# Streaming and retrieval attention into a Swish layer: unit 1 in the packed form of the later units, with a new hand-fixed order

## The chip, the cores and the metric

The kernel runs on one core of a Trainium2 chip. The metric is the time of one execution on the device in microseconds (us). A core has a matrix engine (TensorE, PE in the profile; PEld is its weight load), a vector engine (VectorE, DVE), an activation engine (ScalarE, ACT), a general engine (GpSimd, POOL) and a queue that issues DMAs (SyncE, SP). Each takes its instructions strictly in program order and waits at the first one whose inputs or buffers are not ready.

## The reference

```
scores = q @ k.T / 8                 # batch 4, 8 heads, 768 positions, head size 64
mask   = causal                      # heads 0, 2, 6 ("retrieval")
         causal & (key < 4 or query - key < 64)      # heads 1, 3, 4, 5, 7 ("streaming")
a = softmax(where(mask, scores, -1e9));   y = a @ v
x = y as (4*768, 512);  h = x @ w_in (512 x 2048);  g = h * sigmoid(beta * h)
out = g @ w_out (2048 x 512)
```

All arrays are float32 in memory; the kernel computes in bf16 with float32 sums.

## The kernel before

**Units.** Work is cut into eight units, unit n = 2b + u for batch b and half u of 384 query rows. Each unit loads its part of q, k and v, casts it to bf16, turns q and k (by PE for units 0 to 3, by DMA transposes in blocks for units 4 to 7), forms scores in "rounds" of two PSUM banks, takes exponentials on ACT, masks them on DVE or POOL, sums them and multiplies by v on PE (`pv`, two halves g per unit), and normalises into `xT` on DVE. A streaming head needs only a band: for each chunk of 64 queries two blocks of 64 keys, plus the four sink keys.

**Two forms.** Units 0 and 1 ("early") use five plain rounds for heads 0 and 2, one for heads 1 and 3, one for heads 4 and 5, and rounds for heads 6 and 7 plus a round "k" of sink scores: eleven rounds in unit 1. Their reciprocals are spread over rows by four matmuls (`spread`). From unit 2 on (`n >= RD`) the "packed" form puts several heads' pieces into rounds of up to 512 columns, eight rounds in an odd unit and four in an even one. There the sink keys sit in the oldest rows of a band's own key block: `kp_copy` makes such key blocks (KP), `qd_copy` a copy of head 6 on other partitions (QD), `sink_v` copies the sink rows of v into the shifted and plain v tiles, and three small "edge" DMAs (`load_edge`) bring the v rows that those displaced. Reciprocals R of units 2 to 7 go over DRAM: sums `sc`, turned by DMA into `rec`, reciprocal on DVE, written to `rd`, read back spread over partitions as R.

**The Swish layer.** For each unit `first` runs 16 steps of four matmuls of 384 columns (w_in tile s), each followed by a tanh on ACT (`t`) and a product on DVE (`gT`); `second` runs 48 matmuls of 512 columns (w_out tile 0 to 15, three output row groups) in groups of three. Weights come in four loads of 1 MB for w_in and four for w_out, each cast by POOL in four tiles. PSUM has two pairs of banks for scores (`sp`) and a ring of four banks (`b`). Three staging tiles (`wf`) hold weight loads and the q, k and v blocks of 256 KB (three DMAs to a block triple).

**The order.** Each piece of work is added to a plan with an engine, a cost, what it needs and gives, and ring slots. `SEQUENCE` lists the pieces' numbers in the order in which they are planned and `CHOICE` picks an engine for those that may run on several; `run` gives each piece the planned start that its engine, inputs, slots and a model of the DMA bus allow, and the program is emitted in the order of those starts. So on each engine the order of `SEQUENCE` is the program order, and the costs only place engines against each other and set how many filler matmuls unit 0 gets (`fill`).

Of the kernel before, what the change touches and what calls it, by code (L numbers as in the profile page):

```python
# [19 lines left out]
NQ = 384  # L20
# [4 lines left out]
RD = 2  # L25
KD = 256
# [69 lines left out]
]  # L96
CHOICE = (
    "aagaagaadgaddadadddddgdggdddddaaggaagddagaaddddadaddagdddddaaddggdaaagaggddaadadggggadggaddgggaddgag"
    "daaadaadaadddaaaaaaddddaddaa"
# [102 lines left out]
def kernel(  # L202
# [78 lines left out]
    esk_1, sink_sel = KP[0][:, 0:NQ], KP[2][:, 96:192]  # L281
    blk = KP[1][0:96, 0:NQ].rearrange("p (c n) -> p c n", n=W)
# [97 lines left out]
    def const_blk(eng):  # L380
        cast(eng, blk, sel_k6.unsqueeze(2).to_broadcast([96, CK, W]))
# [116 lines left out]
    def sink_copy(b):  # L498
        VE[b] = vp.tile([128, H - 1, D], BF16, name="VE", bufs=RINGS["VE"])
        dve.tensor_mul(VE[b][0:96], held.pop("sinks")[0:96, D:].rearrange("p (h d) -> p h d", d=D),  # L500
                       sink_own[:, 1:].unsqueeze(2).to_broadcast([96, H - 1, D]))
# [119 lines left out]
    def packed(n):  # L621
        return n >= RD

    def rounds_of(pi, n):
# [31 lines left out]
        def band(h):  # L656
            if n >= RD:
                return strip(h, CK * u, CK * (u + 1), 0)
# [9 lines left out]
        if pi == 3:  # L668
            r = plain(a)
            if u == 0:  # L670
                return [(r[0], band(b)), (r[1], kk)]
# [327 lines left out]
    def pv(x, g):  # L999
# [8 lines left out]
        for t in (2 * g, 2 * g + 1):  # L1008
# [3 lines left out]
            for i, h in enumerate(XT[t] if x.n else (2 * t, 2 * t + 1)):  # L1012
# [14 lines left out]
                else:  # L1027
# [7 lines left out]
                    if x.n < 2:  # L1035
                        continue
# [407 lines left out]
```

## Time and profile before

| | us |
|---|---|
| median of 3 runs | 232.65 (232.5 to 233.43) |
| profiled execution, whole | 233.11 |
| its span from first to last instruction | 231.4 |
| PE busy | 221.7 |
| DVE busy | 154.4 |
| ACT busy | 143.2 |
| POOL busy | 91.0 |

The profile is one execution. Every instruction goes through one helper line (L118), so groups are told apart by tiles: `b<-xT,w_in` is the first product, `b<-w_out,gT` the second, `sp<-QK` scores, `sp<-es,vb` P·V, `b<-es,two` and `b<-es,one` the sums. In a timeline row the first number is the start and the second the length; in brackets stands the time that the engine was idle before it and what ended that. Matmuls are pipelined, so a row's length is longer than the distance to the next one, and costs are read from starts.

### The profile page before, as it was taken

What the parts mean: (1) busy time and instruction counts of PE and PEld (TensorE: products, weight loads), DVE (VectorE), ACT (ScalarE), POOL (GpSimd) and SP (SyncE); (2) the same over time, 40 slices, a digit from 0 to 9 for tenths busy, and PEclk for the clock granted to TensorE, in tenths of its full rate; (3) what the DMA queues carried; (4) which work ended last, traced back from release to release, by engine and by line L of the source; (5) the groups of instructions that cost most, each with busy time, mean ns of one, the idle gap of its engine ahead of it and who ended that gap; (6) DMA issues with size and microseconds to landing.
All of it is one profiled execution on the core that took longest, in us unless ns stands there. A gap on an engine that the chain in (4) does not pass through costs nothing.

```text
span 231.4 us, 6505 instructions
## 1 busy us (share of the span) xinstructions
PE 221.7 (96%) x2577; PEld 128.8 (56%) x2600; DVE 154.4 (67%) x372; ACT 143.2 (62%) x233; POOL 91.0 (39%) x233
## 2 busy tenths in 40 slices
PE   8889999999999979999999999999999999999995
PEld 8656666665544535565555456645555555465543
DVE  5787789877376188886669377764885475467630
ACT  5899988887736158825885277537749445008601
POOL 4717876896763924528453535073000000000000
PEclk9999999999999999999999999999999999999999
DMA  6999999998889999997999899974500015402012
GB/s 188 289 274 358 375 238 323 379 338 203 193 177 224 257 192 216 235 196 142 221 210 217 210 216 252 199 142 126 150 3 0 3 48 146 138 0 91 3 45 91
DMA packets 84264, 42.28 MB, mean 183 GB/s; under 512 B 66042, under 2 KB 77002, under 8 KB 84234
## 3 DMA queue, kind: packets, MB, share of 16 engines
q1 hardware_dynamic: 83962, 41.67, 74.0%
q8 instruction: 20, 0.33, 0.6%
q10 hardware_dynamic: 272, 0.20, 0.3%
q14 instruction: 10, 0.08, 0.1%
HBM read 32.27 MB, written 6.37 MB: 167 GB/s over the span
## 4 chain that ended last, share of the span: by engine, by line
PE 62%; DMA 18%; SPq 7%; POOL 6%; issue 2%; DVE 2%; ACT 1%; POOLq 0%; DVEq 0%
PE b L118 55%; SPq L118 7%; PE sp L118 7%; DMA q2f<-in_q_dram 4%; DMA vf<-in_v_dram 4%; DMA wf<-in_moe_w_out_dram 3%; DMA wf<-in_q_dram 3%; DMA R<-rd 3%; POOL w_out L118 2%; POOL w_in L118 2%; DMA rec<-sc 1%; DVE xT L118 1%; POOL KP L118 1%; POOL c L118 1%; ACT es L118 1%
## 5 line engine op out<-in xcount | busy, mean ns | idle before, releaser
L118 DVE SCALAR_TENSOR_TENSOR gT<-t,b 128x384 bf16<-128x384 f32 x128 | 69.3, 552 | 37.7 <-ACT t L118 32.7
L118 PE MATMUL b<-xT,w_in 128*128 128x384 bf16 x512 | 90.2, 326 | 1.7 <-DVE xT L118 1.6
L118 ACT ACTIVATE t<-b,beta_h 128x384 f32<-128x384 f32 x128 | 72.7, 582 | 28.2 <-PE b L118 22.0
L118 PE MATMUL b<-w_out,gT 128*128 128x512 bf16 (+2 forms) x377 | 85.4, 370 | 2.2 <-issue 1.4
L118 PEld LDWEIGHTS <-w_in 128*128 128x128 bf16 x512 | 48.5, 98 | 36.6 <-issue 1.9
L118 PEld LDWEIGHTS <-gT 128*128 128x128 bf16 x400 | 37.2, 98 | 40.0 <-issue 0.8
L118 ACT ACTIVATE es<-sp 128x1024 bf16<-128x1024 f32 (+4 forms) x50 | 46.0, 945 | 9.4 <-PE sp L118 9.2
L118 ACT ACTIVATE osb<-b 128x512 f32<-128x512 f32 (+2 forms) x14 | 7.9, 567 | 33.3 <-PE b L118 30.8
L118 POOL CAST c<-wf 128x256 bf16<-128x256 f32 x48 | 18.0, 413 | 24.0 <-DMA wf<-in_k_dram 13.4
L118 DVE TENSOR_TENSOR xT<-sp,R 64x384 bf16<-64x384 f32 (+4 forms) x30 | 16.0, 554 | 7.4 <-DMA R<-rd 5.1
L118 POOL COPY KP<-QK 128x24 bf16<-128x24 bf16 (+5 forms) x48 | 11.5, 287 | 18.9 <-DMA QK<-c 15.4
L118 PE MATMUL sp<-QK 64*64 64x64 bf16 (+7 forms) x432 | 17.4, 234 | 0.8 <-ACT es L118 0.7
L118 PEld LDWEIGHTS <-QK 64*64 64x64 bf16 (+1 forms) x432 | 11.0, 105 | 9.4 <-issue 7.5
L118 DVE TENSOR_TENSOR es<-es,mask_c 128x256 bf16<-128x256 bf16 (+3 forms) x39 | 11.6, 315 | 4.7 <-ACT es L118 4.6
L118 POOL CAST vb<-wf 128x512 bf16<-128x512 f32 x18 | 12.1, 690 | 6.5 <-DMA wf<-in_v_dram 6.4
L118 DVE COPY QK<-b 128x384 bf16<-128x384 bf16 (+1 forms) x14 | 8.9, 641 | 7.3 <-PE b L118 7.2
L118 PE MATMUL sp<-es,vb 128*64 128x64 bf16 (+5 forms) x240 | 13.5, 235 | 0.0
L118 DVE TENSOR_SCALAR osb<-b 128x512 f32<-128x512 f32 x11 | 7.5, 680 | 8.4 <-PE b L118 8.4
L118 DVE TENSOR_TENSOR es<-es,mask_s 128x128 bf16<-128x128 bf16 (+7 forms) x28 | 11.9, 438 | 0.0
L118 PEld LDWEIGHTS <-vb 128*64 128x64 bf16 x252 | 11.3, 111 | 0.9
L118 DVE COPY vs<-vb 64x1536 bf16<-64x1536 bf16 (+4 forms) x19 | 9.8, 522 | 1.1 <-POOL vb L118 0.5
L118 POOL CAST w_in<-wf 128x512 bf16<-128x512 f32 x16 | 9.7, 631 | 1.7 <-DMA wf<-in_moe_w_in_dram 1.6
(108 smaller groups left out, 197.2 us busy)
## 6 DMA issues: line engine op xcount, KB each, us to landing
out_dram<-osb SPq DMA_DIRECT2D x23, 256.0 KB, 5.4
wf<-in_v_dram SPq DMA_DIRECT2D x18, 256.0 KB, 4.9
wf<-in_moe_w_in_dram SPq DMA_DIRECT2D x4, 1024.0 KB
wf<-in_moe_w_out_dram SPq DMA_DIRECT2D x4, 1024.0 KB
R<-rd SPq DMA_DIRECT2D x9, 384.0 KB, 5.2
q2f<-in_q_dram SPq DMA_DIRECT2D x16, 192.0 KB, 4.4
wf<-in_q_dram SPq DMA_DIRECT2D x12, 256.0 KB, 5.3
wf<-in_k_dram SPq DMA_DIRECT2D x12, 256.0 KB, 4.7
```

The costliest lines, as they stand in the source:

```text
L118: ins = f(*a, **k)
```

## The change

Unit 1 takes the packed form (`FD = 1`: bands, sinks, KP, QD and edge rows), while its sums and reciprocals stay those of the early units (`n < RD`); its eight rounds are planned as single steps (`SD = 2`), not as bursts of two. The sink scores and the "own" sink rows of v are left to unit 0. The even units' four rounds are cut anew: the bands of heads 4 and 5 leave the first two rounds, so these need no KP, and the masks of the four rounds become 15 instructions instead of 9. A constant (`blk`) moves from a KP tile to an output staging tile. In the plan a block triple is priced at 4.25 instead of 3.65 (q, k) and 3.6 (v), a q/k load at 0.65 instead of 0.62. `SEQUENCE` and `CHOICE` are new throughout.

```diff
+FD = 1
+SD = 2
 SEQUENCE = [
...
 CHOICE = (
...
-        return n >= RD
+        return n >= FD
...
             if pi == 0:
...
-                        ([full(a, 1, 0)] + strip(4, 2, CK, 256), [full(b, 1, 0)] + strip(5, 2, CK, 256))]
+                        ([full(6, 0, 0), full(a, 2, 320), ("z", (6, 1), 0, 448, 0, W)],
+                         [full(b, 1, 0), full(b, 2, 256), ("z", (5, 2), 0, 384, 0, W), ("z", (7, 3), 0, 448, 0, W)])]
             if pi == 3:
-                return [([full(a, 0, 0), ("z", (4, 0), 0, 320, 0, W), ("z", (6, 1), 0, 384, 0, W)] + strip(4, 1, 2, 448),
-                         strip(3, 1, CK, 0) + [("z", (5, 2), 0, 320, 0, W), ("z", (7, 3), 0, 384, 0, W)] + strip(5, 1, 2, 448)),
-                        ([full(0, 2, 0)] + strip(1, 1, CK, 128), [full(2, 2, 0)] + strip(7, 1, CK, 128))]
+                return [([full(0, 1, 0)] + strip(4, 2, CK, 256), strip(3, 1, CK, 0) + strip(5, 1, 4, 320)),
+                        (strip(1, 1, CK, 0) + [("z", (4, 0), 0, 368, 0, W)] + strip(4, 1, 2, 432),
+                         strip(7, 1, CK, 0) + strip(5, 4, CK, 368))]
...
-            return {(0, 0): [("c", 0, 2, 0, W), ("c", 0, 2, 320)], (0, 1): [("c", 0, 2, 0), ("s", 0, 2, 256, 256, 128)],
-                    (3, 0): [("c", 0, 1, 0, W), ("s", 1, 1, 0, 320, W), ("z", 0, 2)],
-                    (3, 1): [("c", 0, 2, 0), ("s", 0, 2, 128, 320 + 3 * NE[0], W)]}[pi, ri]
+            return {(0, 0): [("c", 0, 2, 0, W), ("c", 0, 2, 320)],
+                    (0, 1): [("c", 0, 1, 0, W), ("c", 0, 1, 320), ("z", 0, 1, 448, W, 0), ("c", 1, 1, 0), ("c", 1, 1, 256), ("z", 1, 1, 384, 2 * W, 0)],
+                    (3, 0): [("c", 0, 1, 0), ("s", 0, 1, 256, 256, 128), ("s", 1, 1, 0, 320, W), ("s", 1, 1, 320, 192, W)],
+                    (3, 1): [("s", 0, 2, 0, 320 + 3 * NE[0], W), ("z", 0, 1, 368, 2 * W, W), ("s", 1, 1, 368, 128, 256)]}[pi, ri]
...
                         byj[j].append((e8, piece(x, h, a, W)))
-                if part == len(SUMS) - 1 and a >= sink_from(x.u):
+                        if x.n >= FD:
+                            byj[j].append((e8, x.edge[h][:, SINK * (2 * j + s):SINK * (2 * j + s + 1)]))
+                if part == len(SUMS) - 1 and x.n < FD and a >= sink_from(x.u):
...
-                add("sp", 2.1, lambda i=i: load_block(x, i), dma=3.65, parts=TU,
+                add("sp", 2.1, lambda i=i: load_block(x, i), dma=4.25, parts=TU,
...
-        elif n >= 2:
+        else:
             add("dve", [1.03, 1.37][u], lambda: sink_v(x), needs=[("vs", n)], gives=[("vk", n)])
-        if b and not u:
+        if u == (not b):
             add("sp", 1.25, lambda: load_edge(b), dma=1.0, parts=3, gives=[("vef", b)], take=[("vf", ("e", b), 1)])
...
-        bursts = BURSTS[u] if not early else [[(pi, ri)] for pi in range(NP) for ri in range(len(rounds_of(pi, n)))]
+        bursts = BURSTS[u] if n >= SD else [[r] for bu in BURSTS[u] for r in bu] if n >= FD else [[(pi, ri)] for pi in range(NP) for ri in range(len(rounds_of(pi, n)))]
```

Read out of the numbers of `SEQUENCE`, these are the stretches of the new order that the prediction speaks of (q, k, v with their unit; "wi" and "wo" are the loads of w_in and w_out, one to four, or with a tile number their casts):

```
SP before: unit 0's q, k; some of unit 1's q, k; v0; wi1; the other four q, k of unit 1; wi2; two of unit 2; wi3; wi4; v1; q, k 2; wo1; ... wo4; q, k 3; block q4; q, k 3; v2; v3; sums 2; edge; v4; rd 2; block k4; store; R 2
SP after : unit 0's and all of unit 1's q, k; v0; wi1; wi2; two of v1; wi3; the last of v1; edge; q, k 2; wi4; q, k 2; wo3; wo1; q, k 3; wo2; block q4; wo4; q, k 3; v2; sums 2; v4; edge; rd 2; two stores; block q5; R 2; block k4; ... v3
POOL after, first product: wi tiles 0, 1, 5, 2, 3, 4, 6, 7, 9, 8, a mask, edge cast, 10, 11, ...
POOL after, second product: ... wo tiles 4, 5, 6, 12, 14, 13, 15
PE before around unit 2's P·V: P·V 2, two groups of three of the second product, first step of unit 2
PE after                     : P·V 2, four groups of three of the second product, first step of unit 2
```

More of the change, by code (lines that the diff above doesn't have):

```diff
@@ L380, in const_blk @@
     def const_blk(eng):
-        cast(eng, blk, sel_k6.unsqueeze(2).to_broadcast([96, CK, W]))
+        held["blk"] = op_.tile([128, d_model], F32, name="osb").bitcast(BF16)[0:96, 0:NQ].rearrange("p (c n) -> p c n", n=W)
+        cast(eng, held["blk"], sel_k6.unsqueeze(2).to_broadcast([96, CK, W]))
     def const_sink():
@@ L498, in sink_copy @@
     def sink_copy(b):
-        VE[b] = vp.tile([128, H - 1, D], BF16, name="VE", bufs=RINGS["VE"])
-        dve.tensor_mul(VE[b][0:96], held.pop("sinks")[0:96, D:].rearrange("p (h d) -> p h d", d=D),
+        VE["own"] = vp.tile([128, H - 1, D], BF16, name="VE", bufs=RINGS["VE"])
+        dve.tensor_mul(VE["own"][0:96], held.pop("sinks")[0:96, D:].rearrange("p (h d) -> p h d", d=D),
                        sink_own[:, 1:].unsqueeze(2).to_broadcast([96, H - 1, D]))
@@ L894, in sums @@
                     l, e = byj[j][r]
-                    pe.matmul(x.sm[32 * j:32 * j + 32, 0:W], l, e, start=(part == r == 0),
+                    pe.matmul(x.sm[32 * j:32 * j + 32, 0:e.shape[1]], l, e, start=(part == r == 0),
                               stop=(part == len(SUMS) - 1 and r == len(byj[j]) - 1))
@@ L1000, in pv @@
         vb = v_b[x.b]
-        ve = VE[x.b]
+        ve = VE[x.b if x.n >= FD else "own"]
         o = banks((x.n, "v", g))
@@ L1166, in attention @@
             elif j == 0:
-                add("sp", 2.1, lambda: [load_v(x, j, sp) for j in range(TU)], dma=3.6, parts=TU,
+                add("sp", 2.1, lambda: [load_v(x, j, sp) for j in range(TU)], dma=4.25, parts=TU,
                     gives=[("vf", n, j) for j in range(TU)], take=[("wf", (n, 0), TU)])
@@ L1182, in attention @@
             add("dve", 0.55, lambda: sink_copy(b), needs=[("VKp", b)], gives=[("VK", b)],
-                take=[("VE", b, 4)], drop=[("b", (n, "k"))])
-        elif n >= 2:
+                take=[("VE", "own", 2)], drop=[("b", (n, "k"))])
+        else:
             add("dve", [1.03, 1.37][u], lambda: sink_v(x), needs=[("vs", n)], gives=[("vk", n)])
-        if b and not u:
+        if u == (not b):
             add("sp", 1.25, lambda: load_edge(b), dma=1.0, parts=3, gives=[("vef", b)], take=[("vf", ("e", b), 1)])
             add(("pool", "dve"), (1.03, 0.55), lambda e: cast_edge(b, ENG[e]), port=True, needs=[("vef", b)],
-                gives=[("ve", b)], take=[("VE", b, 4)], drop=[("vf", ("e", b))])
-        vready = ([("vz", n), ("const", "half")] if n >= RD and not u else []) + [("v", n, j) for j in range(TU)] + ([("vk", n), ("ve", b)] if n >= 2 else [("vs", n), ("VK", b)])
+                gives=[("ve", b)], take=[("VE", b, 4 if b else 2)], drop=[("vf", ("e", b))])
+        vready = ([("vz", n), ("const", "half")] if n >= RD and not u else []) + [("v", n, j) for j in range(TU)] + ([("vk", n), ("ve", b)] if n >= FD else [("vs", n), ("VK", b)])
         if u:
@@ L1210, in attention @@
                     needs=[("QK", n, pi, 1), ("const", "zero")], gives=[("KS", n, pi)])
-        elif n >= 2:
+        else:
             kp = [1, 2, 3]
             add(("pool", "dve"), (2.6, 1.15), lambda e: [kp_copy(x, pi, ENG[e]) for pi in kp], port=True,
-                needs=[("QK", v, pi, 1) for pi in kp for v in {n, first_half}] + [("KP", n - 1, pi) for pi in kp if n > 2],
-                gives=[("KP", n, pi) for pi in kp], take=[(f"KP{pi}", n, 1) for pi in kp])
+                needs=[("QK", v, pi, 1) for pi in kp for v in {n, first_half}] + [("KP", n - 1, pi) for pi in kp if n > FD],
+                gives=[("KP", n, pi) for pi in kp], take=[(f"KP{pi}", n, 4 if u and pi == 3 else 1) for pi in kp])
             if True:
@@ L1228, in attention @@
                     drop.append(("KP3", "c"))
-                    cost += 0.12 if not u else 0.0
-                    if u:
-                        take.append(("KP1", "k", 3))
+                    cost += 0.12
                 if packed(n) and not u:
-                    needs += [("QK", n, p, i) for p in ((0, 1, 2, 3) if pi else (0, 2, 3)) for i in range(2)]
-                    needs += [("KP", n, p) for p in ((1, 2, 3) if pi else (2,))]
+                    needs += [("QK", n, p, i) for p in ((0, 3) if (pi, ri) == (0, 0) else (0, 1, 2) if (pi, ri) == (3, 0) else (0, 1, 2, 3)) for i in range(2)]
+                    needs += [("KP", n, p) for p in ((), (1, 2), (1, 2, 3))[pi and 1 + ri]]
                     needs += [("S", n, 0, 1)] if pi else [("QD", n)]
@@ L1268, in attention @@
                         lambda e="dve", pi=pi, ri=ri: masks(x, pi, ri, ENG[e]), port=True,
-                        needs=[("E", n, pi, ri), ("const", "mask" if n < 2 else "new", u)], gives=[("M", n, pi, ri)])
+                        needs=[("E", n, pi, ri), ("const", "mask" if n < FD else "new", u)], gives=[("M", n, pi, ri)])
         M = [("M" if mask_cost(pi, ri, n) else "E", n, pi, ri) for (pi, ri) in rounds]
@@ L1274, in attention @@
                 final = part == len(SUMS) - 1
-                add("pe", [[0.36, 0.26, 0.39], [0.6, 0.23, 0.54]][u][part], lambda part=part: sums(x, part),
+                add("pe", [[0.36, 0.26, 0.39], [0.6, 0.3, 0.6]][u][part], lambda part=part: sums(x, part),
                     needs=[m for m in M if m[2] in pis] + ([] if part else [("const", "two")]) + ([("const", "sink")] if final else []) +
                     ([("sum", n, part - 1)] if part else []), gives=[("sum", n, part)] + ([("sum", n)] if final else []),
-                    take=[] if part else [("b", (n, "s"), 1)], drop=[es_ring(pi, n) for pi in pis] + ([("KP1", "k")] if n == 1 and final else []), mode="sum")
+                    take=[] if part else [("b", (n, "s"), 1)], drop=[es_ring(pi, n) for pi in ([(), (2,), (0, 1, 3)][part] if packed(n) else pis)], mode="sum")
         else:
@@ L1302, in attention @@
         for g in range(2):
[L1303 to L1304 removed]
+            drop = [es_ring(pi, n) for pi in ([(0, 1), (0, 1, 2, 3)] if packed(n) and u else [(0, 3), (0, 3)] if packed(n) else [(0, 1), (2, 3)])[g]] + [("vb", b), ("vs", n), ("VE", b if n >= FD else "own")] + ([("vz", n)] if n >= RD and not u else [])
+            add("pe", ([[0.9, 0.8], [1.06, 0.97]] if n < RD else [[0.57, 0.55], [1.06, 0.77]])[u][g], lambda g=g: pv(x, g),
                 needs=M + vready + ([] if n < RD else [("R", n, 0)]), gives=[("O" if n < RD else "o", n, g)],
@@ L1380 @@
         add(("dve", "pool"), (0.3, 0.45), lambda e, u=u: const_mask_new(u, ENG[e]), gives=[("const", "new", u)], port=True,
-            needs=[("const", "edge", u), ("const", "pair")] +[("M", u, pi, ri) for pi in range(NP) for ri in range(len(rounds_of(pi, u))) if mask_cost(pi, ri, u)] + [("const", "mask", 0)])
+            needs=[("const", "edge", u), ("const", "pair"), ("const", "mask", 0), ("const", "mask", 1)] +
+            [("M", u, pi, ri) for pi in range(NP) for ri in range(len(rounds_of(pi, u))) if u < FD and mask_cost(pi, ri, u)])
         add("dve", [0.67, 0.3][u], lambda u=u: const_mask_s(u), port=True, needs=[("const", "m")], gives=[("const", "mask", u)])
@@ L1387 @@
     add("pool", 1.0, const_pair, needs=[("const", "m")], gives=[("const", "pair")])
-    add("dve", 0.4, const_zero, gives=[("const", "zero")], take=[("KP3", "c", 3)])
+    add("dve", 0.4, const_zero, gives=[("const", "zero")], take=[("KP3", "c", 2)])
     add("dve", 1.05, const_sink, port=True, needs=[("const", "ident"), ("const", "zero")], gives=[("const", "sink")])
@@ L1392 @@
     add(("act", "dve"), (0.45, 0.35), lambda e: const_blk(ENG[e]), port=True, needs=[("const", "low")], gives=[("const", "blk")],
-        take=[("KP2", "c", RD)])
+        take=[("osb", "blk", RD)])
     for s in range(NS // 2):
```

51 lines of the change are left out of this document (22 added, 29 removed), and 108 rows, old and new, of the table SEQUENCE.

## The prediction

> **What bounds the kernel now.** I read the page's head first, then busy time by stretches, then TensorE's timeline, then the waits that end its few gaps.
>
> ```profile
> PE 221.7 (96%) x2577; PEld 128.8 (56%) x2600; DVE 154.4 (67%) x372; ACT 143.2 (62%) x233; POOL 91.0 (39%) x233
> PEclk9999999999999999999999999999999999999999
> DMA  6999999998889999997999899974500015402012
> ```
>
> TensorE (PE) is busy 96% of the span at full clock, and the DMA engines are full from the first microseconds to about 150 us. Busy time by stretches, cut at events named below (columns: window, length, then busy us and instructions of PE, weight load, DVE, ACT, POOL, granted clock, DMA share, GB/s):
>
> ```profile
> 0.00:21.30 21.30, 18.34 (x307) 14.04 (x308) 15.23 (x59) 17.05 (x29) 10.20 (x41) 1.00 0.96 270
> 21.30:41.22 19.92, 19.85 (x325) 12.39 (x323) 17.07 (x36) 17.98 (x34) 14.85 (x33) 1.00 1.03 320
> 41.22:56.90 15.68, 15.57 (x178) 9.19 (x178) 12.07 (x27) 12.67 (x20) 13.62 (x32) 1.00 1.01 310
> 56.90:79.97 23.07, 22.67 (x307) 11.91 (x310) 11.42 (x39) 12.17 (x17) 15.37 (x32) 1.00 0.92 205
> 79.97:84.00 4.03, 2.30 (x10) 0.89 (x12) 2.99 (x5) 0.60 (x1) 0.64 (x2) 1.00 1.18 264
> 84.00:228.70 144.70, 143.00 (x1462) 80.34 (x1477) 95.62 (x211) 82.47 (x135) 36.29 (x97) 1.00 0.62 133
> ```
>
> From 21.3 us on PE is idle 0.07 + 0.11 + 0.40 + 1.73 + 1.70 us. So the time is a start of 21.3 us, then PE's work, and one real hole at 80 to 84 us. In the start and up to 41 us ACT, DVE and DMA are nearly as full as PE, so there an operation added to one of them can hold PE up; after 84 us there is at most 1.7 us to win. The hole (timelines of DVE and PE; last bracket: idle before, and who ended it), with the step before it from the chain that ended last:
>
> ```profile
> 74.95 5.90 DMA R<-rd
> 80.95 2.60 DVE L118 TENSOR_TENSOR xT<-sp,R 64x384 bf16<-64x384 f32 x4 [5.09 <-DMA R<-rd]
> 82.15 0.34 PE L118 MATMUL b<-xT,w_in 128*128 128x384 bf16 x1 [0.80 <-DVE xT L118]
> 82.73 0.32 PE L118 MATMUL b<-xT,w_in 128*128 128x384 bf16 x1 [0.25 <-DVE xT L118]
> 83.60 8.94 PE L118 MATMUL b<-xT,w_in 128*128 128x384 bf16 x54 [0.54 <-DVE xT L118]
> ```
>
> Unit 2's reciprocals R land at 80.9, its normalisation follows, and the first product of unit 2 waits 0.80 + 0.25 + 0.54 = 1.59 us.
>
> **Part 1: PE's work in unit 1.** Unit 1 is to look like units 3, 5 and 7. Rows: unit 1's sums, P·V pair, spreads, unit 2's transposes and the first product of unit 1 from PE's timeline; from the chain, unit 3's P·V pair and a burst of two score rounds of unit 5.
>
> ```profile
> 32.77 1.26 PE L118 MATMUL b<-es,two 128*32 128x64 bf16 x99
> 34.43 1.48 PE L118 MATMUL b<-xT,w_in 128*128 128x384 bf16 x8
> 35.83 0.35 PE L118 MATMUL sp<-KP,VE 96*64 96x384 bf16 x1
> 37.12 0.82 PE L118 MATMUL b<-xT,w_in 128*128 128x384 bf16 x4
> 38.04 0.35 PE L118 MATMUL sp<-KP,VE 96*64 96x384 bf16 x2
> 39.33 0.66 PE L118 MATMUL b<-sc,sel 96*128 96x384 bf16 x3
> 39.83 1.54 PE L118 MATMUL b<-ident,c 128*128 128x128 bf16 x18
> 41.22 6.66 PE L118 MATMUL b<-xT,w_in 128*128 128x384 bf16 x40
> 99.88 1.92 PE sp L118 x49
> 109.01 0.58 PE sp L118 x40
> ```
>
> P·V goes from (37.12 - 35.83) + (39.33 - 38.04) = 2.58 to 1.92: -0.66. Score rounds go from 11 to 8; one is 0.58/2 = 0.29: -0.87. The sums lose six products and gain 30 four-column ones (5 band heads x 6 chunks). Before, 126 products took 34.43 - 32.77 = 1.66, 13 ns each because four column strips overlap: 24 more are +0.3. Together -1.2 us of PE work. [...]
>
> **Part 2: what has to be ready for unit 1's P·V.** New before it: copying sink rows into the bands' oldest rows (DVE), packing KP and QD for unit 1 (DVE), an edge load of three DMAs and its cast (POOL); all q/k loads now stand ahead of the first w_in load.
>
> ```profile
> 24.15 1.72 POOL L118 CAST w_in<-wf 128x512 bf16<-128x512 f32 x3 [0.33 <-DMA wf<-in_moe_w_in_dram]
> 28.01 2.29 POOL L118 CAST w_in<-wf 128x512 bf16<-128x512 f32 x4 [0.68 <-DMA wf<-in_moe_w_in_dram]
> 30.89 0.62 POOL L118 CAST w_in<-wf 128x512 bf16<-128x512 f32 x1 [0.59 <-DMA wf<-in_moe_w_in_dram]
> 31.88 0.61 POOL L118 CAST vb<-vf 128x512 bf16<-128x512 f32 x1 [0.36 <-DMA vf<-in_v_dram]
> q2f<-in_q_dram SPq DMA_DIRECT2D x16, 192.0 KB, 4.4
> wf<-in_moe_w_in_dram SPq DMA_DIRECT2D x4, 1024.0 KB
> L118 DVE COPY vs<-vb 64x1536 bf16<-64x1536 bf16 x8 | 4.7, 591 | 0.4 <-ACT vb L118 0.3
> L118 DVE COPY vs<-vb 4x1344 bf16<-4x1344 bf16 x3 | 1.9, 617 | 0.1
> L118 DVE COPY vb<-vb 4x768 bf16<-4x768 bf16 x3 | 1.6, 541 | 0.1
> L118 DVE COPY vb<-vb 4x192 bf16<-4x192 bf16 x3 | 0.6, 203 | 0.0
> L118 DVE SCALAR_TENSOR_TENSOR gT<-t,b 128x384 bf16<-128x384 f32 x128 | 69.3, 552 | 37.7 <-ACT t L118 32.7
> ```
>
> These casts start when a load lands. So a w quarter takes 30.9 - 28.0 = 2.9 us of the full DMA, a v block 1.0, and a q/k load 192/1024 of 2.9, about 0.55. The second w_in quarter landed at 24.1; the same loads stand ahead of it in the new order, so it stays there, and the first one, which four q/k loads have passed, lands at 24.1 - 2.9 = 21.2 instead of about 19. Then two v blocks (26.2), the third quarter (29.1), the last v block (30.1). On POOL the cast of w_in tile 5 stands ahead of tile 2: PE's third step waits for tile 2 until 25.3. I charge nothing more for that, as the P·V comes later still. Last v block 30.1, cast 0.6, two shifted copies 2 x 0.6, one gT product between 0.55, sink copies 0.62 + 0.54 + 0.20 = 1.4: P·V starts at 34.0, with ten of the sixteen steps of unit 0's first product done. The PSUM ring of four is then full of results that wait for DVE, so PE has nothing to put before it.
>
> Left from there to the point at which before stood at 41.22: P·V 1.9, six steps of 8.94/54 x 4 = 0.66 each, four spreads of (39.83 - 39.33)/3 = 0.17, four transposes of unit 2 at (41.22 - 39.83)/3 = 0.46, and about 0.5 for DVE's backlog: 34.0 + 9.0 = 43.0. That is 1.7 us behind, although PE has less to do.
>
> **Part 3: the last w_out quarter.** In the new SP order it stands behind the q block of unit 4 (three DMAs); before, it stood ahead of it.
>
> ```profile
> 50.61 2.37 POOL L118 CAST w_out<-wf 128x512 bf16<-128x512 f32 x4
> 55.59 1.46 PE L118 MATMUL b<-w_out,gT 128*128 128x512 bf16 x6
> 59.02 0.74 POOL L118 CAST c<-wf 128x256 bf16<-128x256 f32 x2 [3.33 <-DMA wf<-in_q_dram]
> ```
>
> In before all eight quarters, 30 q/k loads, six v blocks and unit 4's q block had landed at 58.9. The new order has the same before the last quarter lands, with one q/k load less and the edge rows more: 58.6. Adding up single prices from part 2 gives 57.8; I take 58.3. Tile 13 of unit 0's second product needs the third cast of that quarter, 0.6 each: 60.1. A tile of 512 columns costs PE 512/384 of the 8.94/54 us of a 384-column one, 0.22, so in before tiles 9 to 14 ran from 55.59 to 56.9, and in the new order tile 14 ends at 60.5. By then the new order has done one transpose (0.46) and unit 2's sums (about 0.7) more, so PE is behind by 60.5 - 56.9 - 1.2 = 2.4 us. By part 2 alone it would be 1.7; the later of the two binds, they don't add.
>
> **Part 4: the hole.** Between unit 2's P·V and its first product the new order has four w_out groups of three tiles instead of two: 12 x 0.22 = 2.6 us, against the 2.60 us that the normalisation took. After the landings of part 3, before still had four block triples (768 KB), one q/k load and one output store to move ahead of R; the new order has three triples, three q/k loads and two stores. At that stretch's 205 GB/s a triple is 3.8 us, a store of 256 KB 1.3, a q/k load 0.55 to 1: in sum about 1.5 us less, from a start 0.6 earlier, so R lands at about 79. P·V of unit 2, 2.4 us later than in before, ends at about 82. So R is there before P·V ends, the normalisation hides behind the four groups, and the 1.59 us go. If R lands after 82 they come back one for one.
>
> **Part 5: the rest.** Unit 2, 4 and 6 get fifteen mask instructions instead of nine.
>
> ```profile
> L118 DVE TENSOR_TENSOR es<-es,mask_c 128x64 bf16<-128x64 bf16 x3 | 1.0, 322 | 0.0
> L118 DVE TENSOR_TENSOR es<-es,mask_s 128x128 bf16<-128x128 bf16 x9 | 2.0, 217 | 0.0
> ```
>
> 18 x 0.22 to 0.32 = 4 to 6 us of DVE in 145 us where it is 66% busy (95.6 of 144.7): nothing on PE as long as sums have slack, 0.5 us if one of the three stages waits. Score products of those units keep their columns. The new order after 84 us shows no load that is later than its user by these prices; unit 4's transposed q/k come within 1 us of theirs. I take 0, between -0.5 and +1.0. The 2.7 us after PE's last product stay.
>
> Sum: +2.4 - 1.6 + 0 = +0.8 us. The profiled execution took 233.11 (span 231.4 and 1.7 around it); its like would take 233.9. It lies 0.46 above the median of 232.65, so for a median I say **233.4**.
>
> **The rivals.** The forecast's own case: the lag at tile 14 lies between 1.4 and 3 and the hole goes, with part 5's bounds: 232.2 to 234.8, chance 0.46.
>
> Faster: the lag doesn't arise. If loads land 2 us earlier than I reckon (the start has 0.96 DMA share, so a little was free) and P·V isn't late, the 1.2 us of saved PE work show and the hole goes too: up to -2.8, or 229.9; half of that lag gives about 230.9. For it: PE has less work, and the new order was given dearer blocks, so it should hold loads back less wrongly. Against it: the DMA is full from 5 to 60 us, and bytes ahead of the last quarter are the same. It decides at tile 13 starting before 58. Chance 0.22.
>
> Slower: R of unit 2 is late again. Its write and read stand behind two output stores and a block triple on SP, each held by a ring of three staging tiles; if R lands after 83.5 the hole stays and the lag is kept: +2.4, with a slower start +3: 235.0 to 235.7. For it: R took 5.9 us to land and the SP queue was blocked by staging tiles. Against: three blocks fewer stand ahead of its first step. Chance 0.27.
>
> The change does not work as it says: unit 1's form saves nothing because PE waits for exponentials between single rounds, and the lag and the hole cancel: 232.6, within the measurement. Chance 0.05.
>
> **How the numbers follow.** About 0.5%, 1.2 us, is what a measurement of this kernel can tell from no change: under 231.5 is faster, over 233.8 slower. Faster: the faster rival. Slower: the slower rival and 0.12 of the forecast's case. Same: the rest. The range, 230.9 to 235.6, holds the forecast's case, most of the slower one and half of the faster one.
>
> **What would show it.** Right: w_in's first cast near 21.3; P·V of unit 1 as rounds with a 24-column product, starting at about 34; PE idle for 1 us or more before tiles 12 to 14 of unit 0's second product, ended by POOL's w_out cast; no idle on xT at unit 2's first product. Wrong: those tiles start before 58, or R ends an idle time on DVE of over 1 us while PE waits, or a hole over 1 us appears after 84.

## The result: 3.8% slower, and the profile after

The changed kernel takes 242.09 us (median of 7 runs, 241.13 to 246.05), the kernel before beside it 232.65 (232.05 to 234.94): the ratio is 1.0378, 95% interval 1.0341 to 1.0415, about 8.8 us. The forecast was 233.4 with a range to 235.6; it was wrong. Medians below are over all runs of a kernel, ratios over those that nothing disturbed, which is why the two can differ by a per cent. The profile shown here is the second one taken of the changed kernel (243.1 us whole, span 241.4), since the first lay 4 us above the median.

Of the page's head, the lines that answer to those of before:

```profile
PE 227.3 (94%) x2691; PEld 132.4 (55%) x2691; DVE 161.1 (67%) x405; ACT 145.8 (60%) x237; POOL 93.1 (39%) x237
PEclk9999997999999999999999999999999999999999
DMA  6999999988659989999889889976900027101022
```

The granted clock has a 7 in the seventh slice, at 36 to 42 us, where before it was full throughout. PE's waits, summed over the span (who waited for whom: total, times, longest), say what ended its idle time:

```profile
PE b L120 <- DVE gT L120: 3.6, 4, 1.3
PE b L120 <- issue: 3.2, 1, 3.2
PE b L120 <- DVE xT L120: 1.1, 1, 1.1
PE b L120 <- POOL w_in L120: 0.8, 1, 0.8
PE b L120 <- DVE c L120: 0.6, 1, 0.6
```

PE's timeline has the same waits in their places:

```profile
18.86 0.34 PE L120 MATMUL b<-ident,c 128*128 128x128 bf16 x3 [0.57 <-DVE c L120]
28.25 2.21 PE L120 MATMUL b<-xT,w_in 128*128 128x384 bf16 x12 [0.76 <-POOL w_in L120]
34.44 0.56 PE L120 MATMUL b<-es,two 128*32 128x64 bf16 x39
38.23 0.27 PE L120 MATMUL b<-es,two 128*32 128x64 bf16 x3 [3.23 <-issue]
59.22 1.46 PE L120 MATMUL b<-xT,w_in 128*128 128x384 bf16 x8 [1.18 <-DVE gT L120]
65.90 0.21 PE L120 MATMUL b<-es,one_z 128*32 128x64 bf16 x4 [1.26 <-DVE gT L120]
91.17 5.04 PE L120 MATMUL b<-xT,w_in 128*128 128x384 bf16 x30
```

The largest is the fourth: between two sums of unit 1, in the middle of a burst, PE does nothing for 3.23 us and waits for nothing that the profile shows ("issue"). I call this the stand. The last row is the first product of unit 2, which before had 1.59 us of idle time in front of it and now has none. Busy time by stretches around the stand (busy us and instructions of PE, weight load, DVE, ACT, POOL; granted clock, DMA share, GB/s):

```profile
34.00:36.00 2.00, 0.99 (x43) 0.56 (x41) 1.42 (x4) 0.80 (x3) 1.94 (x5) 1.00 1.10 348
36.00:38.00 2.00, 0.00 (x0) 0.00 (x0) 0.00 (x0) 0.43 (x1) 1.89 (x5) 0.92 1.03 318
38.00:40.00 2.00, 1.77 (x23) 1.46 (x24) 1.36 (x5) 0.00 (x0) 1.74 (x5) 0.50 1.07 366
40.00:42.00 2.00, 2.00 (x40) 1.66 (x37) 0.98 (x3) 1.27 (x3) 1.84 (x7) 0.72 1.03 364
```

The stand is followed by half clock: (0.08 + 0.50 + 0.28) x 2 = 1.7 us more. So in this execution the stand costs up to 3.2 + 1.7 = 4.9 us. It is the dearest one on record: at the same sums the first profile of the changed kernel stood for 1.77 us, and the variants below that keep this place for 0.8 to 2.3. The half clock is not always there either. Of the seven timed runs, four have a mean granted clock of 0.998 or more and took 241.1 to 242.1 us, two have 0.993 and took 242.1 and 242.4; so the half clock is not what makes the changed kernel slow.

**An account of the whole.** From the trace I add up PE's useful time: each matmul from its start to the next one's start (or its own end), fillers left out, half-clock stretches counted half. Time elapsed less useful time is what was lost so far. The kernel before stands here in a variant with merged fillers (b_less below, whose time is the same), because its trace lacks no matmul; g3 and f64b_nine are experiments below.

| lost by | before (b_less) | after | g3 | f64b_nine |
|---|---|---|---|---|
| 20 us | 9.1 | 11.4 | 11.0 | 11.4 |
| 35 us | 9.6 | 12.5 | 12.7 | 12.3 |
| 45 us | 9.7 | 17.0 | 13.4 | 12.8 |
| 70 us | 10.9 | 19.6 | 14.0 | 12.8 |
| 140 us | 11.2 | 20.9 | 14.7 | 13.4 |
| useful in all | 217.2 | 217.2 | 217.8 | 217.2 |
| span | 231.2 | 241.4 | 235.8 | 233.6 |

After against before, each in one profile: 2.3 us in the first 20, 0.6 up to 35, 4.4 around the stand, 1.4 and 1.0 in the stages of the even units, 0.5 behind the last matmul: 10.2, the difference of these two spans. The medians differ by 9.4 us and the ratio gives 8.8, so one or two of these terms are smaller in a usual execution, the stand first of all.

### The profile page after: what moved, and what is told of

The parts are those of the page before. It is cut to its first block, busy times and chain, and to the rows that moved or that the text cites. A ratio compares the mean times of both kernels' runs of the same rounds, so it can differ in the third digit from the quotient of the medians.

```text
span 244.3 us, 6733 instructions
## 1 busy us (share of the span) xinstructions
PE 226.2 (93%) x2666; PEld 132.4 (54%) x2691; DVE 164.9 (67%) x405; ACT 146.4 (60%) x237; POOL 92.2 (38%) x237
## 4 chain that ended last, share of the span: by engine, by line
PE 68%; DVE 14%; DMA 6%; issue 5%; ACT 4%; SPq 1%; DVEq 0%; ACTq 0%
PE b L120 61%; PE sp L120 7%; DVE es L120 6%; DMA wf<-in_k_dram 2%; DVE gT L120 2%; DMA wf<-in_v_dram 2%; DMA wf<-in_q_dram 2%; DVE xT L120 2%; ACT es L120 1%; SPq L120 1%; DVE vs L120 1%; DVE sc L120 1%; ACT t L120 1%; ACT osb L120 1%; DVE VE L120 1%
## 5 line engine op out<-in xcount | busy, mean ns | idle before, releaser
L120 PE MATMUL b<-xT,w_in 128*128 128x384 bf16 x512 | 92.1, 332 | 2.1 <-DVE gT L120 2.1
L120 PEld LDWEIGHTS <-w_in 128*128 128x128 bf16 x512 | 49.8, 99 | 38.4 <-issue 5.3
L120 POOL CAST c<-wf 128x256 bf16<-128x256 f32 x48 | 18.0, 413 | 35.4 <-DMA wf<-in_k_dram 22.8
L120 ACT ACTIVATE osb<-b 128x512 f32<-128x512 f32 (+2 forms) x16 | 9.0, 571 | 24.0 <-PE b L120 22.6
L120 POOL COPY KP<-QK 128x24 bf16<-128x24 bf16 (+5 forms) x49 | 12.2, 297 | 16.9 <-PE sp L120 7.6
L120 DVE TENSOR_TENSOR es<-es,mask_c 128x128 bf16<-128x128 bf16 (+3 forms) x46 | 13.7, 322 | 4.6 <-ACT es L120 4.3
L120 PEld LDWEIGHTS <-QK 64*64 64x64 bf16 (+1 forms) x429 | 11.4, 107 | 8.4 <-issue 5.1
L120 DVE TENSOR_TENSOR es<-es,mask_s 128x128 bf16<-128x128 bf16 (+7 forms) x35 | 14.3, 429 | 1.8 <-ACT es L120 1.8
L120 POOL CAST vb<-wf 128x512 bf16<-128x512 f32 x18 | 10.7, 624 | 10.5 <-DMA wf<-in_v_dram 10.5
L120 POOL COPY vs<-vb 64x512 bf16<-64x512 bf16 x22 | 12.9, 623 | 0.4
L120 DVE TENSOR_SCALAR osb<-b 128x512 f32<-128x512 f32 x9 | 6.2, 691 | 8.0 <-PE b L120 7.2
L120 PEld LDWEIGHTS <-vb 128*64 128x64 bf16 x255 | 11.2, 111 | 0.7
L120 POOL CAST w_out<-wf 128x512 bf16<-128x512 f32 x16 | 9.3, 620 | 1.5 <-DMA wf<-in_moe_w_out_dram 1.5
```

The lines of the kernel that those rows point to most:

```text
L120: ins = f(*a, **k)
```

## Experiments

Two theories were set against the forecast's own (loads set the pace): **F**, PE is not given its program in time; **M/P**, DVE's masks and copies are held up, by number or by POOL's casts beside them.

**e0_after**, the changed kernel itself, for the profile above.

> The changed kernel as it is, for a profile beside the others: about 242 us, with PE idle for some 2.9 us before unit 1's first round with QD, about 1.8 us before unit 1's P.V, and 1 to 1.3 us each before steps of unit 0 and the sums of unit 2.

243.1 us. The 2.9 us hole before the QD round, which the first profile had, was not there: it comes and goes, the stand does not.

**e1_qd** and **e2_stt**: another instruction form for DVE's work.

```diff
-        dve.tensor_copy(out=x.QD[D:128, 0], in_=x.QK[0:D, 0, 3, NQ:S])
+        dve.scalar_tensor_tensor(out=o, in0=i, scalar=1.0, in1=i, op0=MULT, op1=max)    # unit 1 only
 # e2_stt: also the masks and the product of reciprocals and blk:
-        eng.tensor_mul(e, e, m)
+        dve.scalar_tensor_tensor(out=e, in0=e, scalar=1.0, in1=m, op0=MULT, op1=MULT)
```

> The two copies that make QD for unit 1 are done as max(1.0*x, x) by DVE's scalar_tensor_tensor, the form of the gT products, instead of as copies; nothing else changes. Theory P (DVE's bf16 copy and product forms are kept waiting as long as POOL casts without a gap): the two take about 1 us instead of 3.6, the 2.9 us hole before the QD round goes, and the kernel gains 2 to 2.9 us: about 239.5. Rival L (the landing of loads sets the pace, PE would wait at the next step instead): the hole goes but moves to the next step, 241.5 to 242. Rival S (the copies themselves are long for these shapes): they stay at 3 us or more.

> As before, and all masks on DVE with two free dimensions and unit 0's and 1's product of reciprocals and blk in the scalar_tensor_tensor form too. Theory P: none of them takes over 0.6 us beside POOL's casts, the holes that ended on gT around 62 to 70 us and on sc at 45 us go as well, 236 to 238. Rival L: 240.5 to 242, the same PE steps then wait for loads or POOL's casts.

e1 took 241.7 us (237.5 to 241.8), e2 252.5, ratio 1.0803 [1.0744, 1.0862]. The idea that only the copy form waits fell. e1 itself decides nothing: POOL happened to pause for 0.90 us when the pair came, and the pair took 0.89. In e2 the other form is longer in itself (a mask of 128x736 took 1.12 us instead of 0.55), and PE waited for gT for 7.0 us in all instead of 3.6. DVE's rows for unit 1's two QD copies, with POOL's casts of the same time, in the first profile of the changed kernel, in e0 and (DVE only) in e2:

```profile
24.06 3.63 DVE L120 COPY k2f<-QK 64x384 bf16<-64x384 bf16 x2
22.92 4.52 POOL L120 CAST w_in<-wf 128x512 bf16<-128x512 f32 x8
```

```profile
24.12 0.39 DVE L120 COPY k2f<-QK 64x384 bf16<-64x384 bf16 x2
22.97 1.16 POOL L120 CAST w_in<-wf 128x512 bf16<-128x512 f32 x2
24.36 3.85 POOL L120 CAST w_in<-wf 128x512 bf16<-128x512 f32 x6 [0.23 <-DMA wf<-in_moe_w_in_dram]
```

```profile
24.94 4.29 DVE L120 SCALAR_TENSOR_TENSOR k2f<-QK 64x384 bf16<-64x384 bf16 x2
```

With eight casts in a row (22.92 to 27.44) the copies end at 27.69; with POOL idle for 0.23 us at 24.13, waiting for a load, they take 0.39. The same pair in the other form waits as long, 4.29. So it is POOL's run that holds DVE, not the form. How long it holds is not fixed: in g1 (below) the same two copies, beside eight casts without a gap (23.04 to 27.66), took 1.25 us from 24.19 on, so there DVE got its turn between two casts. In the first profile one of the copies lasted 3.50 us, beside six casts that start 0.56 us apart, until POOL paused.

**e3_nine**: six of fifteen masks left out in each of units 2, 4 and 6.

```diff
-                    (0, 1): [("c", 0, 1, 0, W), ("c", 0, 1, 320), ("z", 0, 1, 448, W, 0), ("c", 1, 1, 0), ("c", 1, 1, 256), ("z", 1, 1, 384, 2 * W, 0)],
+                    (0, 1): [("c", 0, 1, 320), ("c", 1, 1, 0), ("c", 1, 1, 256)],
```

(one entry less in round (3, 1), two in (3, 0))

> Units 2, 4 and 6 leave out six of their fifteen masks, two in the second round of heads 0 and 2 more than the old count would need, so that nine are left as before (those scores are not masked). If the six more instructions cost their own length where PE waits: 2 us less, 240. If they cost nothing, as predicted: 242.

240.0 us, ratio 1.0270 [1.0214, 1.0327] against 1.0378: 2.5 us. The masks are not free. PE's waits on gT fell from 3.6 us to 1.4 in its profile.

**f64, f24, b64**: more PE instructions ahead of everything, to move the stand.

```diff
-        held["gap"] = 3.6
-        fill(bank("fill")[:, 0:128])
+        # 12 (f24: 20) as before, then 79 (f24: 31) tiny ones: net 64 (24) matmuls more
+        pe.matmul(t[32 * (j % 4):32 * (j % 4) + 32, 0:32], blank[:, 0:32], blank[:, 0:32], start=True, stop=True)
```

> The 27 filler matmuls with which PE starts become 12 as they were and 79 tiny ones (32 weights, 32 columns): 64 matmuls, 128 PE instructions, more, before anything else. Theory F: the 1.8 to 3.2 us for which PE stands before the last three sums of unit 1, with nothing that it waits for, is a block of 256 instructions that PE has not been given in time: the block's 16 KB packet lands 5 to 6 us after PE has entered the block before it, and PE uses that up in 4 us, since sums are short. 128 instructions more move the block's limits 64 matmuls up the program, where PE takes 5.6 us or more per block: the stand goes, and with it the 3.4 us of half clock behind it: 4 to 5 us less, 237 to 238. Rival P (PE stands for data, late behind POOL's casts or a load): the stand stays at the same sums, 241.5 to 243.

> The same with 20 and 31: 24 matmuls, 48 instructions, more. Theory F: the limit moves up by 48 instructions only, into the burst of sums, and PE still uses the block up in 4 us: PE stands 24 matmuls earlier in its program, for 1 to 3 us, and the time stays at 241 to 243. Rival P: the stand stays before the last three sums, the same time.

> The kernel before with the 64 more tiny matmuls at its start. Theory F: its limits move so that the block with unit 1's 99 sums in one burst is used up in about 2 us, so that PE stands 1.5 to 3 us in or behind that burst, at about 34 us, and runs at half clock afterwards: 234.5 to 237.5, slower by what made the changed kernel faster. Rival P: 232.5 to 233, as before.

f24 is the clearest. Its stand, and that of a_less and g3 (below), in PE's timelines:

```profile
34.22 0.33 PE L120 MATMUL b<-es,two 128*32 128x64 bf16 x15
36.66 0.47 PE L120 MATMUL b<-es,two 128*32 128x4 bf16 x27 [2.11 <-issue]
```

```profile
33.99 0.62 PE L120 MATMUL b<-es,two 128*32 128x64 bf16 x42
38.04 0.32 PE L120 MATMUL sp<-es,vb 128*64 128x384 bf16 x1 [1.88 <-issue]
```

```profile
32.97 0.27 PE L67 MATMUL b<-es,two 128*32 128x4 bf16 x13 [0.86 <-issue]
33.17 2.15 PE L67 MATMUL b<-xT,w_in 128*128 128x384 bf16 x12
```

The unchanged program stands 3 sums before the end of its burst of 42. With 24 matmuls more in front it stands 27 before it; with 48 fewer (a_less) the 42 sums run through and it stands inside P·V; with 64 more (g3) it stands 13 + 12 matmuls and 39 sums earlier, which is 64. Counted from the start of the program it is the same place each time: behind 1215 records of matmuls and weight loads. It is so in all 13 profiles that have a stand near this place, and two smaller stands lie whole blocks earlier: one of 0.36 us in a_less behind 959 records, which is 256 less, and one of 0.86 us in b64 behind 703, which is 512 less. Data that come late would not move with a filler; a limit in the program does. The page names what has such limits:

```profile
q8 instruction: 20, 0.33, 0.6%
q8 instruction: 21, 0.34, 0.6%
```

Queue q8 (before, after: packets, MB, share) carries packets of 16 KB, 20 and 21 of them for some 5,200 and 5,382 matmuls and weight loads of PE, so about 256 to a packet, which is the distance of the stands. Each packet is set here, by its recorded time, beside the block that PE was in when it landed:

| us | before | after | f24 | a_less | g3 | f64b |
|---|---|---|---|---|---|---|
| PE enters the block | 33.4 | 30.8 | 30.3 | 31.6 | 26.0 | 25.7 |
| packet of the next one has landed | 36.6 | 36.8 | 35.2 | 36.6 | 31.5 | 30.7 |
| PE at the block's end | 39.3 | 35.0 | 34.6 | 36.2 | 32.1 | 31.8 |
| PE goes on | 39.3 | 38.2 | 36.7 | 38.0 | 33.0 | no stand over 0.2 |

PE goes on 1.4 to 1.5 us after the landing in every case of the table that stood. So theory F holds for the cause of the stand: the new form uses up these 256 instructions in 4.2 us instead of 5.9, since they are short ones, and the packet comes 6.0 us after PE entered the block instead of 3.1. The late packet is the larger part. By these numbers a packet that came after 3.1 us would have left a stand of about 0.3 us (30.8 + 3.1 + 1.4 - 35.0), and a block that lasted 5.9 us one of about 1.5 (38.2 - 36.7). Nor do short instructions alone make a stand: at 154.6 us the same profile uses up a block in 4.4 us and runs through, since the packet had landed 1.3 us after PE entered it. Why the packet is late at 36.8 us stays open. That data fill the DMA engines (share 1.10 and 1.03 above) fits, but the share is 0.98 at 154.6 to 159 us too, with 155 GB/s instead of some 350, and no run took the data away.

As times, these three missed. f64: 244.1 us, 1.0467 [1.0415, 1.0519], slower: the stand at the old place was gone, but the first block's packet now came at 6 us instead of 10, PE stood idle for 1.76 and 0.83 us at 7 to 10 us, waiting for casts of unit 0's loads (that these came late because of the packet ahead of them is not shown), the waits on masks grew to 1.57 and 2.34, and two stretches of 3.4 us ran at half clock, from 11.6 and 66.2 us on (mean granted clock 0.986). f24: 243.35, 1.0341 [1.0265, 1.0418]. b64: 234.5, 1.0033 [0.9973, 1.0093], no difference that can be measured; it got a stand of 0.86 us, not at 34 but at 20.8, at the limit of an earlier block. I had reckoned wrongly where a stand would fall in before: the packet for the burst of sums started at 33.6, before PE's matmuls entered the block.

**f64_nine**: f64 with nine masks.

> The 64 more matmuls and, as in the run with nine masks, six masks less in each of units 2, 4 and 6 (those scores are not masked). If the instruction block and the masks are separate losses they add: 237.5 - 2.1 = 235.4. If the masks' cost lies behind the stand: 237.5.

238.2 us, 1.0198 [1.0133, 1.0262]: 5.9 less than f64, whose waits on masks were longer too.

**a_less** and **b_less**: fillers merged, four of 128 columns into one of 512 (changed kernel: 96 instructions less; before: 66).

```diff
-                pe.matmul(dst, blank, blank, start=True, stop=True)
+                pe.matmul(dst, blank, blank.unsqueeze(1).to_broadcast([128, 4, 128]), start=True, stop=True)
```

> PE's filler matmuls of 128 columns are merged, four into one of 512 columns: PE streams the same columns in the same places, with 48 matmuls, 96 PE instructions, less, so the first microseconds stay as they are. Theory F: the limits of the instruction blocks fall 48 matmuls later in the work, where PE takes 5.9 us or more for a block; the stand before unit 1's P.V goes with its half clock, 237 to 238.5, and with it most of the loss. If only its place matters little and data are late there: 241.5 to 243.

> The same merging in the kernel before (33 matmuls less): no block there is used up in under 5 us, so nothing changes: 232.3 to 233.3. Theory F would have to give up if this one were faster by as much as the changed kernel.

a_less: 241.5, 1.0365 [1.0321, 1.0408]; the stand moved (row above) and did not go, with half clock behind it (mean granted clock 0.993). b_less: 233.3, 1.0003 [0.9968, 1.0037], as expected.

**e6** and **g1**: three pieces of the order moved; g1 has the merged fillers too.

```diff
-  DVE: masks of unit 2's second round; gT 9, 11, 10;     PE: sums 2; second product of unit 0 from its tile 12
+  DVE: gT 9, 11, 10; masks of unit 2's second round;     PE: second product, five groups; sums 2
```

> The changed kernel with three pieces of its order moved: on DVE the masks of unit 2's second round behind three gT products that stood behind them, on PE the sums of unit 2 (and ACT's copy of them) behind five more groups of the second product. Theory M (DVE masks wait for a break in POOL's casts, and PE waits for what is behind them): the 1.2 us hole before first-product steps at 58 us and the 1.3 us hole before unit 2's sums shrink by 1.5 to 2.4 us together, 239.5 to 241. Rival: they are made good later or the stand at 35 us grows, 242.

> Both, merged fillers and the three moved pieces: if the losses are separate, 234.5 to 236.5.

e6: 241.4, 1.0350 [1.0299, 1.0401]. Both holes, at 58 and 65 us, went, and 1.7 us came back at 115, on DVE and PE (rows of e6):

```profile
113.79 1.22 DVE L67 TENSOR_TENSOR es<-es,mask_c 128x128 bf16<-128x128 bf16 x1
114.93 1.49 DVE L67 TENSOR_TENSOR es<-es,mask_s 128x256 bf16<-128x256 bf16 x3
116.45 1.02 DVE L67 SCALAR_TENSOR_TENSOR gT<-t,b 128x384 bf16<-128x384 f32 x2
117.06 0.81 PE L67 MATMUL b<-xT,w_in 128*128 128x384 bf16 x4 [2.39 <-DVE gT L67]
```

Unit 4's masks now lie in one piece of 5.4 us ahead of the gT that PE needs. g1: 237.5, 1.0160 [1.0088, 1.0232]; its stand was 1.24 us and no half clock followed. Merged fillers alone (a_less) and the moved pieces alone (e6) gained 0.1 and 0.3% against the changed kernel, both together 2.2%. So these losses don't simply add. Half clock followed the stand in the profiles of a_less and e6 and not in g1's (mean granted clocks 0.993, 0.991 and 1.000), which is worth 1.7 us; what the rest is no run shows.

**f64b**: the 64 matmuls put between 11 and 15 us.

```diff
+        if dst.dtype == F32 and n in (5, 9):        # these fillers: 38 (9) or 20 (5) tiny ones, then 3 or 1 as before
```

> The 64 more matmuls again, now between 11 and 15 us: three fillers of 9, 5 and 5 matmuls become 41, 21 and 21, nearly all of 32 weights and 32 columns; the first 10 us are as in the changed kernel. Theory F: no stand before unit 1's P.V and no half clock there, 236.5 to 238. If the stand only moves on, or late data take its place: 240 to 242.

240.5 us (236.9 to 243.4), 1.0234 [1.0174, 1.0293]: no stand, no half clock in the profile (mean granted clock 1.000), 3.4 us less by the ratio; by the medians of all runs, each less that of before beside it, it is 2.5. The waits on unit 2's masks stayed (1.08 and 1.69).

**e7** and **g2**: POOL is made to pause; g2 adds f64b.

```diff
+        if x.n == 2 and pi == 0 or x.n == 4:        # behind the masks
+            pool.tensor_copy(out=scr[64:96, 0:1], in_=...)        # one column of what DVE has just masked
```

> The changed kernel with seven tiny copies on POOL, each of which reads the result of a DVE mask (unit 2's first two rounds, all rounds of unit 4) or of unit 1's product of reciprocals: POOL must wait there, and DVE gets its turn between POOL's casts. All masks are kept. Theory M: unit 2's masks of 64 columns take 0.5 us in pairs instead of 2.1, the product 0.35 to 0.6 instead of up to 2.3, the 1.2 us hole at 58 us goes: 240 to 241.3. If more masks cost only by their number, nothing changes or POOL's casts come later: 242 to 243.

> f64b and e7 together: 235 to 237 if the losses are separate; the rest to 232.65 would be masks by number and the later start.

DVE's first masks of unit 2 and POOL beside them, in e0 and in e7, and last their like in the kernel before, where POOL was idle from 55.7 to 59.02 us:

```profile
56.06 2.13 DVE L120 TENSOR_TENSOR es<-es,mask_c 128x64 bf16<-128x64 bf16 x2
56.28 1.73 POOL L120 CAST w_out<-wf 128x512 bf16<-128x512 f32 x3
```

```profile
53.62 0.32 DVE L120 TENSOR_TENSOR es<-es,mask_c 128x64 bf16<-128x64 bf16 x2
54.61 0.18 POOL L120 COPY scr<-es 32x1 bf16<-32x1 bf16 x1 [1.18 <-ACT t L120]
```

```profile
56.45 0.62 DVE L118 TENSOR_TENSOR es<-es,mask_c 128x128 bf16<-128x128 bf16 x3
```

2.13 us became 0.32, and PE's 1.18 us hole went. So theory P (POOL's casts hold the masks up) is shown for the mechanism. For the time it is not: e7 took 241.4, 1.0352 [1.0304, 1.0400], which can't be told from the changed kernel, as POOL's last w_out casts then came later (PE idle 0.74 on them); g2, with 241.0 and 1.0303 [1.0265, 1.0341], was not better than f64b alone.

**s26**: the filler of 26 ahead of the first scores made tiny, count unchanged.

> The changed kernel with the filler of 26 matmuls ahead of its first scores made of 26 tiny ones (32 weights, 32 columns), the count of instructions unchanged. In the changed kernel the filler ran from 5.95 to 7.99 us, and the first scores, whose q and k were there at 6.35, behind it. If the filler costs the start: first scores at 6.4 to 6.6, PE's useful work at 20 us 1 to 1.5 us ahead of the changed kernel's 8.6, and 240.5 to 241. If loads and ACT set the start: PE waits for the next step instead, useful work at 20 us within 0.4, 242.

Scores began at 6.28 instead of 7.99, yet useful work at 20 us was 8.8 against 8.6, and the time 241.7, 1.0341 [1.0285, 1.0397]. The filler does not set the start; PE then waited for ACT's and DVE's casts of q and k (0.84 and 0.88).

**g3** and **f64b_nine**: f64b with e6's order (all masks kept), and f64b with nine masks.

> The 64 more matmuls between 11 and 15 us and the three moved pieces (unit 2's second masks and its sums later), all masks kept. f64b gave 239.8 in its profiled run, the moved pieces took 2.4 us of holes away at 58 and 65 us and gave 1.7 back at 115 us: 236.5 to 238.5 if separate, 240 if f64b's gain depended on them.

> The 64 more matmuls between 11 and 15 us with six masks less in each even unit from unit 2 on (those scores are not masked). If separate: f64b less 2 to 2.5 us, 236.5 to 238. What remains above 232.65 then is the start and the order of the first 45 us.

g3: 237.3, 1.0152 [1.0099, 1.0206]. f64b_nine: 236.5, 1.0119 [1.0066, 1.0173]. The plainest measure of the block's limit is g3 against e6, which has the same order: 1.0350 against 1.0152, 4.6 us; f64b_nine against e3_nine gives 3.5. Moving the block's limit and taking the masks out of PE's way recovers 1.0378 - 1.0152 = 2.3% (5 us), leaving masks out 2.6% (6 us). None of the versions beats the kernel before. What remains, 3.5 us by the ratio, is mostly the 2 us of the start (table), whose cause stays open: the new order of the first loads and casts was changed in no run.

## Why the prediction was wrong

The sum said +0.8 us, and 8.8 were measured. The step that failed is the list of what can hold PE up: PE's work, loads, and engines by busy time. PE's own program was not on it, and no rival named it. DVE's masks were, and were put at nothing. A third part, some 2 us lost in the first 20, had no term in the sum.

- **PE's program as a transfer.** The forecast (parts 1 and 2) made unit 1's PE work denser in short instructions and charged only their own time. They are delivered in blocks beside the data (q8, 21 packets of 16 KB), and here they ran out: 3.2 us, and 1.7 at half clock, in the profiled run, and 2.5 to 4.6 us by the runs that moved the limit (f64b against the changed kernel, g3 against e6). The page had q8, and the row of 99 sums in 1.26 us showed how fast a block can go; I read neither as a limit. Neither shows how late a packet can come.
- **Part 5, masks at nothing (-0.5 to +1.0).** Measured: 2.5 us (e3) and 2.7 (f64b_nine against f64b, 1.0119 and 1.0234). The 66% busy time of DVE is an average, and over the wrong stretch: unit 2's masks lie at 56 us, before the 84 us at which it begins. The even units' masks come in one piece ahead of gT, and beside POOL's casts they took several times their length (a pair 2.13 us in e0, 0.32 in e7); in before POOL was idle beside unit 2's. Three of PE's four waits on gT (1.18, 1.26 and 0.69 us) stand behind masks of units 2 and 4, and without six masks (e3) the first two are 0.84 and 0.41 and the third is gone; the fourth (0.50) is there with nine masks as well (0.55 in f64b_nine). "0.5 us if one of the three stages waits" was the right idea, but more than one stage waited, and each for longer.
- **Part 1, PE's work: -1.2.** Measured 0 in all (217.2 and 217.2), and about -0.9 in the forecast's own terms: scores fell by 1.0 (forecast 0.87), P·V of unit 1 went from 2.58 us to 2.1 to 2.3 (e0, f24) where I had 1.92, and unit 1's sums cost 0.5 where I had 0.3. What I left alone made up for it: the second product's rows add up to 0.6 more and the spreads to 0.3. In a burst the sums do go at 14 ns each (e0: 60 from 30.39 to 31.21 us), near the 13 of before; where the other 0.2 us went is not shown.
- **Part 2, P·V at 34.0.** PE was there at 35.0, the last input, the cast of the edge rows, at 35.4 (a_less began P·V at 34.54). Right to about a microsecond, in part by luck: the sink copies, which I had last, ended at 35.0, and the edge cast, which ended after them, had no price in the forecast. What I put nothing for, the first 20 us, lost 2.3.
- **Part 3, the last w_out quarter.** Forecast 58.3; POOL's wait for it ended at 59.3. PE came to its tiles later still, so the lag of 2.4 us never showed; only in e7 and g3 did PE wait for w_out casts (0.74 and 0.40 us).
- **Part 4, the hole on R.** Right. P·V of unit 2 is followed by twelve matmuls that hide the normalisation, and the first product starts at 91.17 with no idle time. So the slower rival (R late again) was wrong too: a loss came, but not by R.
- **The bounds of the forecast's own case.** A lag of 1.4 to 3, less 1.6, with part 5's -0.5 to +1.0, gives 232.0 to 235.1 and not 232.2 to 234.8. It makes no difference to the miss.

## What to carry to other kernels

Count PE's instructions as well as its time: where a few hundred short ones come together while DMA is full (here 256 records in 4.2 us at a DMA share of 0.96 to 1.10), check in the profile when the instruction packets land and how long PE takes for a block, and test it by shifting the program with small fillers. Read a mask or copy on DVE by what POOL does beside it, not by its length elsewhere; a long run of POOL work without a pause was a wait for DVE here (3.50 us for a copy of 0.19 to 0.49), and what stood behind the copy waited too (PE 2.87 us). An operation costs nothing only if it is not ahead of what the bound engine needs next.

## What was new about the hardware

- PE went on 1.4 to 1.5 us after a 16 KB instruction packet had landed, in the four stands of the table and in the first profile of the changed kernel (landed at 40.02, PE on at 41.54), all five behind 1215 records. Each packet took 0.9 to 1.6 us itself in before and in that profile. In these blocks, at whose end PE stood, the next packet landed 4.2 (first profile) to 6.0 us (e0) after PE's entry; in another block of e0 it took 1.3 (at 154.6).
- A stand of 1.9 us (a_less) was followed by 3.4 us at half clock, one of 2.1 (f24) was not: the mean granted clocks of these profiled runs are 0.993 and 1.000. In e0 half clock began at 37.7 us, behind 2.7 us without a matmul, and lasted 3.4. In the first profile of the changed kernel it began at 27.3, behind 2.4 us, and lasted 6.8; behind the stand of 1.77 us there (39.77 to 41.54) the clock stayed full. The stretches of that profile's clock records, 20.48, 6.83 and 211.63 us, and the full clock of 225.28 in before are 6, 2, 62 and 66 times 3.413 us. Why one stand counts and another doesn't is not shown.
- QD copies and masks, whose operands all lie in SBUF, waited on DVE beside POOL's casts. In the first profile of the changed kernel one copy of 64x384 took 3.50 us, the others 0.19 to 0.49, and a mask of 128x64 took 2.03, another of 128x64 0.21; the two copies of unit 1 in the other form took 4.29 (e2). The gT products, which read PSUM, kept their 0.55 us: on average 0.550 for the 28 that lay beside casts, 0.551 for the other 100.
- In the same profile DVE, ACT, POOL and SP started all of their 405, 237, 237 and 170 instructions in the program's order. On PE some matmuls of a burst, and some weight loads, changed places with neighbours, so the "strictly" of the first section is too much for PE.
